# An attention block gated by an MLP, one core: the last head group in a new order, and another way through its last two units

## The chip, the cores and the metric

The kernel runs on one core of one Trainium2 chip. The metric is the device time of one execution in microseconds. The engines are called PE (TensorE), DVE (VectorE), ACT (ScalarE), POOL (GpSimd) and SP (SyncE, here only a DMA queue).

## The reference

`x` has 2048 tokens of 512 features. Its layer norm `xn` feeds two branches. One is attention with 32 heads of 128 features over a cache of 2048 keys, the other an MLP whose output gates the first.

```python
q = (xn @ wq).reshape(B, Sq, H, Dh)                       # 32 heads, Dh = 128
scores = einsum("bhqd,bhkd->bhqk", q, k_cache) * Dh**-0.5
o = einsum("bhqk,bhkd->bhqd", softmax(scores), v_cache)
s = o.reshape(B, Sq, H * Dh) @ wo                         # 4096 -> 512
h = gelu(layernorm(xn) @ w1), each quarter of its features shifted by 1 or 2 tokens
x1 = xn + h @ w2
g = silu(x1 + gelu(layernorm(x1) @ w3) @ w4)
out = x + s * g
```

Inputs and output are bf16.

## The kernel before

The MLP branch comes first; its result, twice the gate, lies in `xall` (16 token tiles of 128). Most of the time is then attention. It is cut into 128 units: 8 head groups (`g`) x 4 query blocks of 512 tokens (`qt`) x 4 heads (`hh`), in this order. Below, the 16 units of the last group are numbered 0 to 15. A unit has 8 slots (`p`), each with 256 keys. In slot `p` the kernel issues, for every engine in the order that is written (`pin` keeps it):

- `s_slot`: two matmuls of scores, transposed (keys on the partitions), into one of two double banks `psS`, and ACT's exp of both (`pT`). No maximum is subtracted.
- `pv_slot`, five slots later (`LAG`): two matmuls that add to the head's output `o`, transposed, in a bank of `psO`.
- p 0, 1: the q projection for the next unit into bank "xa" of `psX`; p 2: DVE copies it to `qT` (`q_copy`).
- p 4, p 6 and p 0 of the next unit: DVE adds up the four `pT` pieces into `acc` (`add_first`, `add_next`, `add_last`; the last one folds it twice more, to 512 columns).
- p 3: `sums` for the unit before. Four matmuls with a vector of ones sum over the partitions, into bank "xa"; DVE takes the reciprocal; SP writes it to DRAM (`dr`), and at p 4 `bcast` reads it back, spread over all partitions (`rb`).
- p 2: `norm` for the unit two before: DVE multiplies `o` by `rb` into `oT`.
- p 4, 5, 6: if a query block of a group is complete, one of its four token tiles goes through Wo (`wo_mm`, four matmuls, one per head, into bank "xm") and `wo_post`. DVE adds the result to `sacc`; in the last group DVE then multiplies by half of `xall` and adds `x` (loaded by POOL's DMA queue, `fin_load`), and SP writes the tile out.

One unit takes one token tile of the block that was finished before, so that in the last group five tiles are left when the units end; a loop does them one after the other.

PSUM has eight banks: two double ones for scores, two for `o`, "xa" and "xm".

Of the kernel before, what the change touches and what calls it, by code (L numbers as in the profile page):

```python
# [8 lines left out]
ACT = mybir.ActivationFunctionType  # L9
ALU = mybir.AluOpType  # L10
FP32 = mybir.dt.float32
BF16 = mybir.dt.bfloat16
# [5 lines left out]
def kernel(  # L18
# [15 lines left out]
    nc = tc.nc  # L34
    P = nc.NUM_PARTITIONS

    x2d = A_x.flatten_outer_dims()
    out2d = out.flatten_outer_dims()
    Sq, D = x2d.shape
    _, H, Sk, Dh = A_k_cache.shape  # L40
# [4 lines left out]
    QT = Sq // 512  # L45
# [5 lines left out]
    HG = 4  # L51
    NG = H // HG

    SPU = KC // 2
    LAG = 5
# [6 lines left out]
    pin = tc.keep_in_program_order  # L62

    def pool(name, bufs=1, space=None, **kw):
        if space is not None:
            kw["space"] = space
        return tc.tile_pool(name=name, bufs=bufs, **kw)

    ent = ctx.enter_context
    const = ent(pool("const"))  # L70
    xnT = const.tile([P, DC, Sq], BF16, name="xnT")
    xall = const.tile([P, NT, D], BF16, name="xall")
    ones_t = const.tile([P, 1], BF16, name="ones_t")
    nhalf = const.tile([P, 1], FP32, name="nhalf")
    mv1 = const.tile([P, NT, nc.vector.BN_AGGR_DIM], FP32, name="mv1")
    mv2 = const.tile([P, NT, nc.vector.BN_AGGR_DIM], FP32, name="mv2")
# [10 lines left out]
    smp = ent(pool("smp", 4))  # L87
    tokp = ent(pool("tok", 4))
    drp = ent(pool("drp", 4, bass.MemoryType.DRAM))
    psS = ent(pool("psS", 2, PSUM))  # L90
    psO = ent(pool("psO", 2, PSUM))
    psX = ent(pool("psX", 1, PSUM))
# [12 lines left out]
    def mm(out, lhsT, rhs, start, stop):  # L105
        pin(nc.tensor.matmul(out=out, lhsT=lhsT, rhs=rhs, start=start, stop=stop))  # L106

    pin(nc.vector.memset(warm[:], 0.0))
    pin(nc.vector.memset(ones_t[:], 1.0))
    pin(nc.vector.memset(nhalf[:], -0.5))  # L110
    pin(nc.gpsimd.iota(diag[:], pattern=[[-1, P]], base=0, channel_multiplier=1,
                       allow_small_or_imprecise_dtypes=True))
    pin(nc.vector.tensor_scalar(
        out=ident[:], in0=diag[:], scalar1=0.0, scalar2=None, op0=ALU.is_equal))

    units = [(g, qt, hh) for g in range(NG) for qt in range(QT) for hh in range(HG)]
    NU = len(units)
    NS = NU * SPU
    kTs, vBs, wqs, wos, oTs, st = {}, {}, {}, {}, {}, {}
# [136 lines left out]
    def q_mm(u, dcs, tag="xa"):  # L256
        g, qt, hh = units[u]
        if dcs[0] == 0:
            st[u] = dict(psq=psX.tile([P, 512], FP32, tag=tag, name="ps_q"))
        for dc in dcs:  # L260
            mm(st[u]["psq"][:], wqs[g * HG + hh][:, dc, :],
               xnT[:, dc, qt * 512:(qt + 1) * 512], dc == 0, dc == DC - 1)
# [9 lines left out]
    def s_slot(u, p):  # L272
        g, qt, hh = units[u]
        s = st[u]
        sps = psS.tile([P, 2, 512], FP32, name="ps_s")
        for j in range(2):
            kc = 2 * p + j
            kv = kTs[g * HG + hh].rearrange("d (i p j) -> d i j p", p=P, j=KJ)
            mm(sps[:, j, :], kv[:, kc // KJ, kc % KJ, :], s["qT"][:], True, True)
        if p % 2 == 0:  # L280
            s.setdefault("pT", []).append(pB.tile([P, 4, 512], BF16, tag="pT", bufs=4, name="pT"))
        jj = 2 * (p % 2)
        pin(nc.scalar.activation(  # L283
            out=s["pT"][-1][:, jj:jj + 2, :], in_=sps[:], func=ACT.Exp, scale=SCALE))

    def add_first(u):
        s = st[u]
        s["acc"] = pB.tile([P, 4, 512], BF16, tag="acc", bufs=2, name="acc")
        pin(nc.vector.tensor_tensor(  # L289
            out=s["acc"][:], in0=s["pT"][0][:], in1=s["pT"][1][:], op=ALU.add))  # L290

    def add_next(u, i):
        a = st[u]["acc"]
        pin(nc.vector.tensor_tensor(out=a[:], in0=a[:], in1=st[u]["pT"][i][:], op=ALU.add))  # L294
# [7 lines left out]
    def pv_slot(u, p):  # L302
        g, qt, hh = units[u]
        s = st[u]
        if p == 0:
            s["o"] = psO.tile([P, 512], FP32, tag="ps_o", name="ps_o")
        pT = s["pT"][p // 2]
        for j in range(2):
            kc = 2 * p + j
            mm(s["o"][:], vBs[g * HG + hh][:, kc, :], pT[:, 2 * (p % 2) + j, :], kc == 0, kc == KC - 1)  # L310
# [10 lines left out]
        pin(nc.sync.dma_start(out=s["dr"][:], in_=rc[:]))  # L321

    def bcast(u):
        st[u]["rb"] = pB.tile([P, 512], FP32, tag="rb", bufs=2, name="rb")
        pin(nc.sync.dma_start(
            out=st[u]["rb"][:], in_=st[u]["dr"][:].rearrange("p j -> (p j)").partition_broadcast(P)))

    def norm(u):
        g, qt, hh = units[u]
        s = st.pop(u)  # L330
        if hh == 0:
            oTs[(g, qt)] = pB.tile([P, HG, 512], BF16, tag="oT", bufs=2, name="oT")
        pin(nc.vector.tensor_tensor(  # L333
            out=oTs[(g, qt)][:, hh, :], in0=s["o"][:], in1=s["rb"][:], op=ALU.mult))

    wo_box = {}
    sacc = {}
# [2 lines left out]
        wos[h] = pB.tile([P, D], BF16, tag="wo", bufs=2 * HG, name="wo_h")  # L340
        pin(nc.sync.dma_start(out=wos[h][:], in_=A_wo[h * Dh:(h + 1) * Dh, :]))

    def wo_mm(g, t, hhs, ps=None):
        if hhs[0] == 0:
            wo_box[0] = psX.tile([P, D], FP32, tag="xm", name="ps_wo") if ps is None else ps
        oT = oTs[(g, t // 4)]
        ts = t % 4
        for hh in hhs:
            mm(wo_box[0][:], oT[:, hh, ts * P:(ts + 1) * P], wos[g * HG + hh][:], hh == 0, hh == HG - 1)

    fin = {}

    def fin_load(t):
        xl = tokp.tile([P, D], BF16, tag="ta", bufs=10, name="xl")
        pin(nc.gpsimd.dma_start(out=xl[:], in_=xsrc[t]))  # L355
        fin[t] = xl

    def wo_post(g, t):
        ps = wo_box.pop(0)
        if g == 0:  # L360
            sacc[t] = pS.tile([P, D], FP32, tag="sacc", bufs=NT, name="sacc")
            pin(nc.vector.tensor_copy(out=sacc[t][:], in_=ps[:]))
            return
        sa = sacc[t][:]
        pin(nc.vector.tensor_tensor(out=sa, in0=ps[:], in1=sa, op=ALU.add))  # L365
        if g < NG - 1:
            return
        xl, gl = fin.pop(t), xall[:, t, :]
        pin(nc.vector.scalar_tensor_tensor(  # L369
            out=gl, in0=sa, scalar=0.5, in1=gl, op0=ALU.mult, op1=ALU.mult))  # L370
        pin(nc.vector.tensor_tensor(out=xl[:], in0=gl, in1=xl[:], op=ALU.add))  # L371
        pin(nc.sync.dma_start(out=out2d[t * P:(t + 1) * P, :], in_=xl[:]))

# [120 lines left out]
    pB = left.enter_context(pool("pB", reuse_waits="tile"))  # L496
# [6 lines left out]
    for g in range(NG - 1):  # L503
        b = (g * QT + QT - 1) * HG
        for hh in range(HG):
            h = (g + 1) * HG + hh
# [24 lines left out]
            at(n + 4, lambda: gate_silu(t, th["a"]))  # L531

    wo_todo = deque()
    for n in range(NS + 3 * SPU):
        u, p = divmod(n, SPU)
        if u < NU:
            g, qt, hh = units[u]
            s_slot(u, p)
        m = n - LAG
        if 0 <= m < NS:  # L540
            pv_slot(*divmod(m, SPU))
        if p in (0, 1) and 4 * HG - 1 <= u < NU - 1:
            q_mm(u + 1, (2 * p, 2 * p + 1))
        if p == 0 and 1 <= u <= NU:
            add_last(u - 1)
        if p == 2 and 4 * HG - 1 <= u < NU - 1:
            q_copy(u + 1)
        if p == 2 and 2 <= u <= NU + 1:
            norm(u - 2)
            if units[u - 2][2] == HG - 1:  # L550
                gg, qq = units[u - 2][:2]
                wo_todo.extend((gg, 4 * qq + ts) for ts in range(4))
                if gg == NG - 1:
                    fin_load(4 * qq)
        if p == 3 and 1 <= u <= NU:
            sums(u - 1)
        if p == 4 and 1 <= u <= NU:
            bcast(u - 1)
        if p in (4, 5) and wo_todo:
            wo_mm(*wo_todo[0], (0, 1) if p == 4 else (2, 3))  # L560
        if p == 6 and wo_todo:
            gg, t = wo_todo.popleft()
            wo_post(gg, t)
            if gg == NG - 1 and t % 4 < 3:
                fin_load(t + 1)
        if p == 4 and u < NU:
            add_first(u)
        if p == 6 and u < NU:
            add_next(u, 2)
        held_mm(n)  # L570
        for fn in todo.pop(n, ()):
            fn()
        if not held and not todo.get(n + 1) and pS is None and n >= 4 * SPU + 5:
            right.close()
            pS = right.enter_context(pool("pS", side="right", reuse_waits="tile"))
    while wo_todo:
        gg, t = wo_todo.popleft()
        wo_mm(gg, t, (0, 1, 2, 3))
        if t not in fin:
            fin_load(t)  # L580
        wo_post(gg, t)
    left.close()
    right.close()

# [29 lines left out]
```

## Time and profile before

| | us |
|---|---|
| three runs | 1289.19, 1289.25, 1290.49; median 1289.25 |
| the profiled execution | 1289.44 |
| its span in the profile | 1287.6 |
| busy: PE, ACT, DVE, POOL | 1257.4, 1054.8, 942.5, 47.5 |
| granted PE clock, mean | 0.991 |

The span runs from the first to the last recorded instruction or transfer; the profiled execution is 1.84 us longer. Some helpers record for many callers: all matmuls and weight loads stand under L106, and are told apart by their tiles (`ps_s` scores, `ps_o` output, `ps_wo` Wo, `ps_sum` sums, `ps_q` projection). L283 is the exp, L289 `add_first`, L294 `add_next`, L299 and L300 the folds, L267 the q copy, L319 the reciprocal, L321 and L325 the write and the read of the round trip, L333 `norm`, L365, L369 and L371 the three instructions of `wo_post`, L372 the output. L167 and L168 are POOL's part of the layer norm, L177 its last DVE instruction, all in the first 76 us. A timeline line has the start, the length, the engine, the line, the operation, and in brackets the idle time before it and what ended it.

### The profile page before, as it was taken

What the parts mean: (1) busy time and instruction counts of PE and PEld (TensorE: products, weight loads), DVE (VectorE), ACT (ScalarE), POOL (GpSimd) and SP (SyncE); (2) the same over time, 40 slices, a digit from 0 to 9 for tenths busy, and PEclk for the clock granted to TensorE, in tenths of its full rate; (3) what the DMA queues carried; (4) which work ended last, traced back from release to release, by engine and by line L of the source; (5) the groups of instructions that cost most, each with busy time, mean ns of one, the idle gap of its engine ahead of it and who ended that gap; (6) DMA issues with size and microseconds to landing.
All of it is one profiled execution on the core that took longest, in us unless ns stands there. A gap on an engine that the chain in (4) does not pass through costs nothing.

```text
span 1287.6 us, 16764 instructions
## 1 busy us (share of the span) xinstructions
PE 1257.4 (98%) x6128; PEld 609.6 (47%) x6252; DVE 942.5 (73%) x1316; ACT 1054.8 (82%) x1101; POOL 47.5 (4%) x115
## 2 busy tenths in 40 slices
PE   7999999999999999999999999999999999999995
PEld 3444444444444444444444444444444444444442
DVE  6721467777777777777777777777777777778886
ACT  4344779998888888888888888888888888888882
POOL 5320000000000000000000000000000000000000
PEclk9999999999999999999999999999999999999997
DMA  9293122443144522452145423451244323442211
GB/s 209 45 172 74 21 46 50 82 91 67 41 74 77 97 34 51 90 96 46 48 83 77 79 42 59 90 95 33 55 91 78 62 51 72 85 82 43 65 43 49
DMA packets 170771, 91.57 MB, mean 71 GB/s; under 512 B 124928, under 2 KB 153088, under 8 KB 170688
## 3 DMA queue, kind: packets, MB, share of 16 engines
q1 hardware_dynamic: 166464, 84.72, 34.3%
q0 software_dynamic: 1824, 4.98, 1.7%
q8 instruction: 49, 0.80, 0.3%
q10 hardware_dynamic: 2400, 0.79, 0.2%
q14 instruction: 34, 0.28, 0.1%
HBM read 67.63 MB, written 2.36 MB: 54 GB/s over the span
## 4 chain that ended last, share of the span: by engine, by line
PE 89%; DVE 6%; DMA 2%; ACT 1%; issue 1%; POOL 0%; another core or an unknown queue 0%; SPq 0%; DVEq 0%; ACTq 0%
PE ps_s L106 36%; PE ps_o L106 35%; PE ps_wo L106 8%; PE ps_q L106 7%; DVE acc L294 2%; PE ps_m L106 2%; PE ps_sum L106 1%; ACT pT L283 1%; DVE sacc L365 1%; DVE xall L369 1%; DVE acc L299 1%; DMA kT<-in_A_k_cache_dram 1%; DVE qT L267 0%; DVE xl L371 0%; DMA xnT<-xall 0%
## 5 line engine op out<-in xcount | busy, mean ns | idle before, releaser
L283 ACT ACTIVATE pT<-ps_s 128x1024 bf16<-128x1024 f32 x1024 | 993.1, 1026 | 135.3 <-PE ps_s L106 130.4
L106 PE MATMUL ps_o<-pT,vb 128*128 128x512 bf16 x2030 | 605.0, 379 | 3.3
L106 PE MATMUL ps_s<-qT,kT 128*128 128x512 bf16 x1986 | 596.8, 380 | 3.9 <-ACT pT L283 1.2
L294 DVE TENSOR_TENSOR acc<-acc,pT 128x2048 bf16<-128x2048 bf16 x256 | 312.3, 1220 | 72.3 <-ACT pT L283 71.2
L106 PEld LDWEIGHTS <-kT 128*128 128x128 bf16 x2048 | 222.0, 113 | 203.0 <-issue 6.1
L106 PEld LDWEIGHTS <-vb 128*128 128x128 bf16 x2048 | 199.9, 98 | 225.7
L289 DVE TENSOR_TENSOR acc<-pT 128x2048 bf16<-128x2048 bf16 x128 | 156.8, 1225 | 51.2 <-ACT pT L283 51.2
L106 PE MATMUL ps_wo<-wo_h,oT 128*128 128x512 bf16 x509 | 154.5, 387 | 6.2 <-DVE sacc L365 3.1
L365 DVE TENSOR_TENSOR sacc<-ps_wo,sacc 128x512 f32<-128x512 f32 x112 | 77.4, 691 | 89.5 <-PE ps_wo L106 88.7
L106 PE MATMUL ps_q<-xnT,wq_h 128*128 128x512 bf16 x481 | 141.6, 379 | 0.2
L299 DVE TENSOR_TENSOR acc<-acc 128x1024 bf16<-128x1024 bf16 x128 | 88.5, 691 | 4.4
L333 DVE TENSOR_TENSOR oT<-ps_o,rb 128x512 bf16<-128x512 f32 x128 | 87.3, 682 | 2.6 <-DMA rb<-dr 2.6
L106 PEld LDWEIGHTS <-oT 128*128 128x128 bf16 x512 | 50.4, 99 | 70.2 <-issue 7.6
L106 PEld LDWEIGHTS <-wq_h 128*128 128x128 bf16 x512 | 50.0, 98 | 60.4 <-issue 0.3
L267 DVE CAST qT<-ps_q 128x512 bf16<-128x512 f32 x112 | 76.3, 682 | 0.0
L300 DVE TENSOR_TENSOR acc<-acc 128x512 bf16<-128x512 bf16 x128 | 54.4, 425 | 4.4
L106 PEld LDWEIGHTS <-acc 128*128 128x128 bf16 x512 | 37.6, 116 | 34.2 <-issue 4.0
L355 POOL DMA_DIRECT2D xl<-in_A_x_dram x16 | 8.7, 543 | 1137.4 <-DMA out_dram<-xl 1014.3
L106 PE MATMUL ps_s<-xn2T,w_sb 128*128 128x512 bf16 x220 | 48.6, 379 | 0.2
L106 PEld LDWEIGHTS <-w_sb 128*128 128x128 bf16 x304 | 30.0, 99 | 39.1 <-issue 7.7
L234 ACT ACTIVATE h2T<-ps_s 128x1024 bf16<-128x1024 f32 x28 | 28.7, 1024 | 24.0 <-PE ps_s L106 23.3
L319 DVE RECIPROCAL rc<-ps_sum 128x4 f32<-128x4 f32 x128 | 23.2, 181 | 21.3 <-PE ps_sum L106 7.2
(45 smaller groups left out, 332.2 us busy)
## 6 DMA issues: line engine op xcount, KB each, us to landing
rb<-dr SPq DMA_DIRECT2D x128, 256.0 KB, 4.3
vb<-in_A_v_cache_dram SPq DMA_DIRECT2D x64, 256.0 KB, 4.4
wo_h<-in_A_wo_dram SPq DMA_DIRECT2D x32, 128.0 KB, 4.2
wq_h<-in_A_wq_dram SPq DMA_DIRECT2D x28, 128.0 KB, 4.5
w_sb<-in_B_w_dram SPq DMA_DIRECT2D x9, 256.0 KB, 5.4
kT<-in_A_k_cache_dram SPq DMA_TRANSPOSE x128, 4.4
xl<-in_A_x_dram POOLq DMA_DIRECT2D x16, 128.0 KB, 2.3
dr<-rc SPq DMA_DIRECT2D x128, 2.0 KB, 1.4
```

The source lines that it names most:

```text
L106: pin(nc.tensor.matmul(out=out, lhsT=lhsT, rhs=rhs, start=start, stop=stop))
L234: pin(nc.scalar.activation(out=h2[c, f][:], in_=ps[:], func=ACT.Gelu_apprx_tanh))
L267: pin(nc.vector.tensor_copy(out=qT[:], in_=st[u].pop("psq")[:]))
L283: pin(nc.scalar.activation(out=s["pT"][-1][:, jj:jj + 2, :], in_=sps[:], func=ACT.Exp, scale=SCALE))
L289: pin(nc.vector.tensor_tensor(out=s["acc"][:], in0=s["pT"][0][:], in1=s["pT"][1][:], op=ALU.add))
L294: pin(nc.vector.tensor_tensor(out=a[:], in0=a[:], in1=st[u]["pT"][i][:], op=ALU.add))
L299: pin(nc.vector.tensor_tensor(out=a[:, 0:2, :], in0=a[:, 0:2, :], in1=a[:, 2:4, :], op=ALU.add))
L300: pin(nc.vector.tensor_tensor(out=a[:, 0, :], in0=a[:, 0, :], in1=a[:, 1, :], op=ALU.add))
L319: pin(nc.vector.reciprocal(out=rc[:], in_=ps[:]))
L333: pin(nc.vector.tensor_tensor(out=oTs[(g, qt)][:, hh, :], in0=s["o"][:], in1=s["rb"][:], op=ALU.mult))
L365: pin(nc.vector.tensor_tensor(out=sa, in0=ps[:], in1=sa, op=ALU.add))
L369: pin(nc.vector.scalar_tensor_tensor(out=gl, in0=sa, scalar=0.5, in1=gl, op0=ALU.mult, op1=ALU.mult))
```

## The change

The units of the last group are put in another order: heads 0 to 2 of query blocks 2 and 3, then all heads of blocks 0 and 1, then head 3 of blocks 2 and 3. So the two last units (`UA`, `UB`; units 14 and 15) are one head each of blocks 2 and 3. For these two blocks (`LATE`) the Wo tiles in the units sum three heads only, and are already multiplied by the gate and have `x` added, into `sacc`. The last head's share is added later.

In the last ten units a unit does a second tile, at p 0 to 2, where more than one waits (by the queue this is units 6, 8, 9 and 12). In the last group the addition of `x` is POOL's, not DVE's.

For the two last units there is no round trip through DRAM. Their outputs are copied unscaled to SBUF (`late_o`; DVE for the first, ACT in two halves for the second), go through Wo, which puts tokens on the partitions, and are scaled there by the reciprocal as a per-partition scalar. The sums for that come out of PE with tokens on the partitions (`late_sums`): 16 matmuls of one column over `acc` for unit 14, without the folds; for unit 15, 16 over `acc` of its first two pieces, 16 over the third and 16 over the fourth. The vector holds twos, which makes the factor one half. The Wo results of unit 15 go into the two bank pairs of the scores and "xa"; its first tile is scaled by ACT and multiplied and added by POOL, the other three are DVE's. Outputs go out from SP's and ACT's queues.

The four tiles of block 1 are done during unit 15 and the five slots after it, between the matmuls.

```diff
-    units = [(g, qt, hh) for g in range(NG) for qt in range(QT) for hh in range(HG)]
+    units = [(g, qt, hh) for g in range(NG - 1) for qt in range(QT) for hh in range(HG)]
+    LATE = (QT - 2, QT - 1)
+    units += [(NG - 1, qt, hh) for qt in LATE for hh in range(HG - 1)]
+    units += [(NG - 1, qt, hh) for qt in range(QT - 2) for hh in range(HG)]
+    units += [(NG - 1, qt, HG - 1) for qt in LATE]
...
-        st[u]["rb"] = pB.tile([P, 512], FP32, tag="rb", bufs=2, name="rb")
+        st[u]["rb"] = pB.tile([P, 512], FP32, tag="rb", bufs=7, name="rb")
...
-            mm(wo_box[0][:], oT[:, hh, ts * P:(ts + 1) * P], wos[g * HG + hh][:], hh == 0, hh == HG - 1)
+            mm(wo_box[0][:], oT[:, hh, ts * P:(ts + 1) * P], wos[g * HG + hh][:], hh == 0, hh == hn - 1)
...
-    def wo_post(g, t):
+    def wo_post(g, t, eng=nc.vector):
...
+        if t // 4 in LATE:
+            pin(nc.vector.scalar_tensor_tensor(
+                out=sa, in0=sa, scalar=0.5, in1=gl, op0=ALU.mult, op1=ALU.mult))
+            pin(nc.gpsimd.tensor_tensor(out=sa, in0=sa, in1=xl[:], op=ALU.add))
+            return
...
-        pin(nc.vector.tensor_tensor(out=xl[:], in0=gl, in1=xl[:], op=ALU.add))
+        pin(eng.tensor_tensor(out=xl[:], in0=gl, in1=xl[:], op=ALU.add))
...
+    def late_sums(u, src, first, last):
+        ps = st[u]["sum"]
+        for j in range(4):
+            for i, a in enumerate(src):
+                mm(ps[:, j:j + 1], a[:, j * P:(j + 1) * P], twos_t[:],
+                   first and j == 0 and i == 0, last and j == 3 and i == len(src) - 1)
...
+    def late_wo(u, ts, ps):
+        h = units[u][0] * HG + units[u][2]
+        mm(ps, st[u]["ou"][:, ts * P:(ts + 1) * P], wos[h][:], True, True)
+
+    def late_mul(u, ts, ps):
+        t = 4 * units[u][1] + ts
+        tm = pB.tile([P, D], FP32, tag="rb", bufs=7, name="tm")
+        pin(nc.vector.scalar_tensor_tensor(
+            out=tm[:], in0=ps, scalar=st[u]["rc"][:, ts:ts + 1], in1=xall[:, t, :],
+            op0=ALU.mult, op1=ALU.mult))
+        return tm
+
+    def late_act(u, ts, ps):
+        t = 4 * units[u][1] + ts
+        tm = pB.tile([P, D], FP32, tag="rb", bufs=7, name="tm")
+        pin(nc.scalar.activation(out=tm[:], in_=ps, func=ACT.Identity, scale=st[u]["rc"][:, ts:ts + 1]))
+        pin(nc.gpsimd.tensor_tensor(out=tm[:], in0=tm[:], in1=xall[:, t, :], op=ALU.mult))
+        return tm
+
+    def late_out(u, ts, tm, eng, queue):
+        t = 4 * units[u][1] + ts
+        y = tokp.tile([P, D], BF16, tag="ta", bufs=10, name="y")
+        pin(eng.tensor_tensor(out=y[:], in0=tm[:], in1=sacc[t][:], op=ALU.add))
+        pin(queue.dma_start(out=out2d[t * P:(t + 1) * P, :], in_=y[:]))
...
+    def wo_slot(part, eng=nc.gpsimd):
+        gg, t, hn = wo_todo[0]
+        if part < 2:
+            wo_mm(gg, t, (0, 1) if part == 0 else tuple(range(2, hn)), hn)
+            return
+        wo_todo.popleft()
+        wo_post(gg, t, eng)
...
+        extra = u >= NU - 10 and len(wo_todo) > 1
...
+        if p == 0:
+            twice = extra
+        if twice and p < 3:
+            wo_slot(p)
...
+    for p in range(SPU + LAG):
+        if p < SPU:
+            s_slot(UB, p)
+        pv_slot(*divmod(UB * SPU + p - LAG, SPU))
+        if p == 0:
+            add_next(UA, 3)
+        if p == 1:
+            late_ps(UA)
+            late_sums(UA, [st[UA]["acc"][:, i, :] for i in range(4)], True, True)
+            late_rc(UA)
...
+        if p in (3, 6, 8, 10):
+            wo_tile(nc.gpsimd if p < 10 else nc.vector)
+        if p == 4:
+            late_o(UA, nc.vector)
+            add_first(UB)
+        if p in (5, 7):
+            late_tile(UA, p - 5, bank(psX, "xa"))
+            late_tile(UA, p - 4, bank(psO, "ps_o"))
+        if p == 9:
+            w = [psS.tile([P, 2, 512], FP32, name="ps_s") for _ in range(2)]
+            st[UB]["sum"] = w[0][:, 0, 0:4]
+            late_sums(UB, [st[UB]["acc"][:, i, :] for i in range(4)], True, False)
+        if p == 10:
+            late_sums(UB, [st[UB]["pT"][2][:, i, :] for i in range(4)], False, False)
+        if p == 11:
+            late_sums(UB, [st[UB]["pT"][3][:, i, :] for i in range(2)], False, False)
+        if p == 12:
+            late_o(UB, nc.scalar)
+            late_sums(UB, [st[UB]["pT"][3][:, i, :] for i in range(2, 4)], False, True)
+    late_rc(UB)
+    ws = [w[0][:, 1, :], w[1][:, 0, :], w[1][:, 1, :], bank(psX, "xa")]
+    for ts in range(4):
+        late_wo(UB, ts, ws[ts])
+    tm = late_act(UB, 0, ws[0])
+    late_out(UB, 0, tm, nc.gpsimd, nc.scalar)
+    tms = {ts: late_mul(UB, ts, ws[ts]) for ts in (1, 2)}
+    late_out(UB, 1, tms[1], nc.vector, nc.sync)
+    tms[3] = late_mul(UB, 3, ws[3])
+    late_out(UB, 2, tms[2], nc.vector, nc.scalar)
+    late_out(UB, 3, tms[3], nc.vector, nc.sync)
```

More of the change, by code (lines that the diff above doesn't have):

```diff
@@ L73 @@
     ones_t = const.tile([P, 1], BF16, name="ones_t")
+    twos_t = const.tile([P, 1], BF16, name="twos_t")
     nhalf = const.tile([P, 1], FP32, name="nhalf")
@@ L109 @@
     pin(nc.vector.memset(ones_t[:], 1.0))
+    pin(nc.vector.memset(twos_t[:], 2.0))
     pin(nc.vector.memset(nhalf[:], -0.5))
@@ L341, in load_wo, with wo_mm @@
         pin(nc.sync.dma_start(out=wos[h][:], in_=A_wo[h * Dh:(h + 1) * Dh, :]))
-    def wo_mm(g, t, hhs, ps=None):
+    def wo_mm(g, t, hhs, hn):
         if hhs[0] == 0:
-            wo_box[0] = psX.tile([P, D], FP32, tag="xm", name="ps_wo") if ps is None else ps
+            wo_box[0] = psX.tile([P, D], FP32, tag="xm", name="ps_wo")
         oT = oTs[(g, t // 4)]
@@ L372, in wo_post, with late_ps, late_rc @@
         pin(nc.sync.dma_start(out=out2d[t * P:(t + 1) * P, :], in_=xl[:]))
+    def late_ps(u):
+        st[u]["sum"] = psX.tile([P, 4], FP32, tag="xa", name="ps_sum")[:]
+    def late_sums(u, src, first, last):
[4 more added lines that the diff above has]
+                   first and j == 0 and i == 0, last and j == 3 and i == len(src) - 1)
+    def late_rc(u):
+        rc = smp.tile([P, 4], FP32, tag="rl", bufs=2, name="rl")
+        pin(nc.vector.reciprocal(out=rc[:], in_=st[u]["sum"]))
+        st[u]["rc"] = rc
@@ new lines, in late_o @@
+    def late_o(u, eng):
+        s = st[u]
+        s["ou"] = pB.tile([P, 512], BF16, tag="ou", bufs=2, name="ou")
+        for c in (slice(0, 256), slice(256, 512)):
+            if eng is nc.scalar:
+                pin(eng.activation(out=s["ou"][:, c], in_=s["o"][:, c], func=ACT.Identity))
+            elif c.start == 0:
+                pin(eng.tensor_copy(out=s["ou"][:], in_=s["o"][:]))
+    def late_wo(u, ts, ps):
+        h = units[u][0] * HG + units[u][2]
+        mm(ps, st[u]["ou"][:, ts * P:(ts + 1) * P], wos[h][:], True, True)
@@ L533, with norm_queue @@
     wo_todo = deque()
-    for n in range(NS + 3 * SPU):
+    def norm_queue(u):
+        norm(u)
+        gg, qq, hh = units[u]
+        late = gg == NG - 1 and qq in LATE
+        if hh == HG - 1 - late:
+            wo_todo.extend((gg, 4 * qq + ts, HG - late) for ts in range(4))
+            if gg == NG - 1:
+                fin_load(4 * qq)
+    UA, UB = NU - 2, NU - 1
+    def wo_slot(part, eng=nc.gpsimd):
[5 more added lines that the diff above has]
+        wo_post(gg, t, eng)
+        if gg == NG - 1 and t % 4 < 3 and t + 1 not in fin:
+            fin_load(t + 1)
+    for n in range(UB * SPU):
         u, p = divmod(n, SPU)
-        if u < NU:
-            g, qt, hh = units[u]
-            s_slot(u, p)
+        extra = u >= NU - 10 and len(wo_todo) > 1
+        s_slot(u, p)
         m = n - LAG
@@ L541 @@
             pv_slot(*divmod(m, SPU))
-        if p in (0, 1) and 4 * HG - 1 <= u < NU - 1:
+        if p in (0, 1) and 4 * HG - 1 <= u:
             q_mm(u + 1, (2 * p, 2 * p + 1))
-        if p == 0 and 1 <= u <= NU:
+        if p == 0 and 1 <= u:
             add_last(u - 1)
-        if p == 2 and 4 * HG - 1 <= u < NU - 1:
-            q_copy(u + 1)
[L548 to L555, printed above, removed]
+        if p == 0:
+            twice = extra
+        if twice and p < 3:
+            wo_slot(p)
+        if p == 2 and 4 * HG - 1 <= u:
+            q_copy(u + 1)
+        if p == 2 and 2 <= u:
+            norm_queue(u - 2)
+        if p == 3 and 1 <= u:
             sums(u - 1)
-        if p == 4 and 1 <= u <= NU:
+        if p == 4 and 1 <= u:
             bcast(u - 1)
[L559 to L566, printed above, removed]
+        if p in (4, 5, 6) and wo_todo:
+            wo_slot(p - 4)
+        if p == 4:
             add_first(u)
-        if p == 6 and u < NU:
+        if p == 6:
             add_next(u, 2)
@@ L575, with wo_tile, late_tile, bank @@
             pS = right.enter_context(pool("pS", side="right", reuse_waits="tile"))
[L576 to L581, printed above, removed]
+    def wo_tile(eng):
+        for part in range(3):
+            wo_slot(part, eng)
+    def late_tile(u, ts, ps):
+        late_wo(u, ts, ps)
+        late_out(u, ts, late_mul(u, ts, ps), nc.gpsimd, nc.sync)
+    def bank(pl, tag):
+        return pl.tile([P, D], FP32, tag=tag, name="ps_w")[:]
@@ new lines @@
+    w = None
+    for p in range(SPU + LAG):
[8 more added lines that the diff above has]
+            late_rc(UA)
+        if p == 2:
+            norm_queue(UB - 2)
+            for t in range(1, 4):
+                fin_load(4 * (QT - 3) + t)
+        if p in (3, 6, 8, 10):
+            wo_tile(nc.gpsimd if p < 10 else nc.vector)
+        if p == 4:
+            late_o(UA, nc.vector)
[14 more added lines that the diff above has]
+            late_sums(UB, [st[UB]["pT"][3][:, i, :] for i in range(2, 4)], False, True)
```

## The prediction, made before the changed kernel was run

> **What bounds the kernel now.** I read the page first, then DVE's reciprocals (L319, one for each unit, so their distance is the length of a unit), then the chain of waits over the last 60 us, then the timelines of POOL and DVE. The unit numbers 0 to 15 are those of the last head group.
>
> The page: the share of the chain by engine.
>
> ```profile
> PE 89%; DVE 6%; DMA 2%; ACT 1%; issue 1%; POOL 0%; another core or an unknown queue 0%; SPq 0%; DVEq 0%; ACTq 0%
> ```
>
> PE bounds the kernel almost everywhere. The DVE timeline, reciprocals of units 4 to 7:
>
> ```profile
> 1159.92 0.18 DVE L319 RECIPROCAL rc<-ps_sum 128x4 f32<-128x4 f32 x1
> 1168.69 0.18 DVE L319 RECIPROCAL rc<-ps_sum 128x4 f32<-128x4 f32 x1
> 1177.95 0.17 DVE L319 RECIPROCAL rc<-ps_sum 128x4 f32<-128x4 f32 x1
> 1187.06 0.17 DVE L319 RECIPROCAL rc<-ps_sum 128x4 f32<-128x4 f32 x1
> ```
>
> A unit takes 8.77 us up to unit 5, then 9.26 once, then 9.10. The 8.77 is PE's own: ten back-to-back PV matmuls spread over 2.32 us, the last of them 0.38, so one comes every 0.2156 us, and 40 of them make 8.62; the four sums take the other 0.15, 0.036 each. From unit 5 on a tile of the last group costs DVE three instructions (L365, L369, L371) instead of one. The chain of waits through unit 13, start, length and work:
>
> ```profile
> 1241.23 0.27 PE ps_sum L106 x4
> ...
> 1243.68 0.45 PE ps_wo L106 x2
> ...
> 1244.15 0.70 DVE sacc L365
> ...
> 1244.88 0.70 DVE xall L369
> ...
> 1245.60 0.42 DVE xl L371
> 1246.02 1.15 DVE acc L294
> ...
> 1247.27 1.24 DVE acc L294
> ...
> 1248.53 0.70 DVE acc L299
> ...
> 1249.59 0.69 DVE qT L267
> ```
>
> It is a loop: PE's sums to the end of Wo 2.92 us, then DVE 0.73 + 0.72 + 0.42 for the tile, 1.25 and 1.26 for the two acc adds, 0.72 + 0.34 for the folds, 0.74 for the q copy, which frees the bank that the next sums need. Sum 9.10, and PE waits for it. The end of the chain:
>
> ```profile
> 1269.50 4.14 DMA rb<-dr
> ...
> 1275.80 1.88 PE ps_wo L106 x4
> ...
> 1284.45 0.42 DVE xl L371
> ```
>
> After the last scores come a DMA round trip (L321 1.38 us, L325 4.14) and five Wo tiles, each waiting for one bank. From the sums of unit 14 (1250.33) to the end of the span (1287.6) are 37.3 us.
>
> **The change, unit by unit.** The span is 1287.6 us, the profiled execution 1289.44, the median 1289.25: changes of the span are added to 1289.25. About 0.2% (2.6 us) can be told from no change.
>
> *Order of units, loads.* The same instructions, and the heads 0 to 2 start in the same units. Head 3 is first used in unit 9 instead of 3, so its K and V have more time. Cost 0. Seven rb buffers and one memset (0.06 us at the start) cost 0.
>
> *One DVE add less per tile.* L371 (0.42) goes to POOL, so the loop with one tile falls to 8.68, under PE's 8.77. A tile of three heads needs one matmul less: chain 8.46, PE 8.55.
>
> *Two tiles in one unit* (6, 8, 9, 12). The extra tile puts 0.73 + 0.72 = 1.45 on the loop ahead of the q copy, and 3 or 4 matmuls on PE. Chain 8.46 + 1.45 = 9.91 with three heads (PE 9.20), 8.68 + 1.45 = 10.13 with four (PE 9.63): DVE decides.
>
> *Sum for units 6 to 14, nothing colliding:* 9.91 three times (6, 8, 9), 8.55 twice (7, 10), 8.05 for unit 11 (no tile; PE 7.91, and exps back to back come every 0.92 us, which holds the bare slots), 10.13 (12), 8.77 twice (13, 14): 82.55 us. Before it is 1250.79 - 1168.69 = 82.10. So 12 tiles instead of 9 are done here for +0.4.
>
> *The POOL add.* No row has its like. From below: POOL's iota writes 128 elements per partition in 0.237 us, a memset of 5 takes 0.09, so 1.17 ns an element, and 512 make 0.69 with the fixed part if reads come free; from above, three streams in turn (two read, one written), 0.09 + 3 x 0.60 = 1.89. I take 1.25, between them, since a write may run beside a read. The Trainium skill's "GPSIMD Engine Reference", section 3.1, has 2.6 cycles an element for a two-input add, an estimate of 1.1 us here; no run here shows it yet, and by it each wait below is 0.15 shorter.
>
> What it does to DVE hangs on who gets SBUF first. The timelines of DVE and POOL in the first stage:
>
> ```profile
> 6.63 0.38 DVE L177 TENSOR_SCALAR xall<-xin,mv,rs 128x512 bf16<-128x512 bf16 x1
> ```
>
> ```profile
> 4.57 0.22 POOL L167 TENSOR_SCALAR ve<-mv 128x1 f32<-128x1 f32 x1 [3.21 <-DVE mv L173]
> ...
> 6.80 0.29 POOL L167 TENSOR_SCALAR ve<-mv 128x1 f32<-128x1 f32 x1 [0.48 <-DVE mv L173]
> ...
> 7.92 0.35 POOL L167 TENSOR_SCALAR ve<-mv 128x1 f32<-128x1 f32 x1 [0.18 <-DVE mv L173]
> ```
>
> Alone, L167 takes 0.22. The one at 6.80 meets L177 (to 7.01) and ends at 7.09; the one at 7.92 meets L177 (7.78 to 8.19) and ends at 8.27: POOL finished 0.08 after DVE both times, so it waited. In the loop DVE starts its next instruction 0.02 to 0.05 after the one before. I conclude that POOL, ready just after L369, finds the acc adds and folds in its way and is served when DVE reads PSUM. With one tile that is the q copy and the norm: 1249.59 to the next acc add at 1250.93 is 1.34 us, and 1.25 + 0.08 fits. With two tiles it is the second tile's sacc add (0.73), so the product after it waits 0.60. Four times (into units 6, 8, 9, 12): +2.4. Units 6 to 14: +0.4 + 2.4 = +2.8.
>
> Queues: POOL's x load (0.54, landing 2.3 later) stands behind the add, which delays only POOL. On SP the output of a (q block 0) tile waits for POOL's add, and the next unit's dr and rb wait behind it; today rb is issued at 1252.39, lands about 4.3 later (1256.7), and its norm starts at 1258.70, so 2.0 us of delay are covered.
>
> *The tail*, from the sums of unit 14. Removed: the round trip before the last two heads, their norms, the folds, five serial Wo tiles. Steps:
> 1. Sums 0.27 and four bare slots at 0.92: unit 15 starts at 3.95.
> 2. PE's program for unit 15 up to the last sums: 62 matmuls x 0.2156 = 13.4; 64 sums in runs. Such a run loads weights each time: three loads take 0.18, so 0.06 each, 3.8 (by the 0.036 of above 2.3; kept for the range). Waits: the 16 sums of unit 14 need its last acc add (its exp ends 0.7 into unit 15, add 1.25, so 0.3 late), the first late Wo needs the copy behind a tile's two instructions (0.4). 17.9, at 21.9.
> 3. Reciprocal 0.2, late Wo to the second bank 0.6: 22.7. ACT's copy (0.60 for the whole tile by L269) lies beside the last sums.
> 4. DVE: three products and three adds at 0.72: 27.0. ACT and POOL do the fourth tile: 0.6 + 2 x 1.25, ready by 26, hidden.
> 5. Today L371 ends at 1284.87 and the span at 1287.6, so 2.7 for the output: 29.7. The middle of the tail has 11 us of DVE work in 12, so collisions with POOL's seven adds may show: I put 0.8, giving 30.5.
> Tail: 30.5 - 37.3 = -6.8.
>
> Sum: +2.8 - 6.8 = **-4.0 us: 1285.3.**
>
> **Rivals.**
>
> *A. No collision at all* (DVE acc adds and POOL don't hinder each other; the rows above show only a tensor_scalar in POOL's way). +0.4 - 7.6 = -7.2: 1282.1; with cheap sums 1280.6.
>
> *B. POOL is next as soon as it waits, and then DVE waits (slower).* The add, ready after L369, waits through the first acc add; at its end POOL goes ahead, and the second acc add waits 1.25 + 0.08 = 1.33. It is on the loop wherever a tile is finished at the end of a unit: intervals 6, 7, 8, 9, 10, 12, 13, 14. 8 x 1.33 = 10.6; +0.4 + 10.6 = +11.0; the tail loses 2 (-5.6). +5.4: 1294.7. It decides from (7.2 - 2) / 8 = 0.65 us of wait per add; with the add's bounds, 0.69 and 1.89, the result is +1.0 to +10.6. For it: POOL did wait on DVE, so some way is shared; against: no DVE instruction in the first stage is seen waiting for POOL (L177 takes 0.38 to 0.41 throughout). The rule of the Trainium skill, "SBUF — State Buffer", section "Who interferes with whom", speaks for it: a DVE instruction with two SBUF inputs and a POOL instruction that reads SBUF exclude each other, and the first to start holds the way to its end. The acc adds have two such inputs, the q copy and norm do not; the trace agrees that POOL waits (0.08 after L177's end), and shows no DVE wait.
>
> *C. They share.* Each slows the other by half, 0.67 a tile end: +0.4 + 5.4 - 6.6 = -0.8: 1288.4.
>
> **How the numbers follow.** Forecast 0.35, A 0.22, B 0.35, C 0.08. Faster by over 0.2%: forecast and A, 0.57. Same: C, 0.08. Slower: B, 0.35. The forecast's own range is 1283.8 to 1287.3 (sums 1.5 less; collisions 2 more). The range must take in A and most of B: 1281.0 to 1296.0, leaving out the cheap end of A and B above 1.5 us an add, together under 0.2. Forecast and B are equally likely, but A lies on the forecast's side.
>
> **What the changed profile would show.** Reciprocals of units 6, 8, 9, 12 about 10.5 us after the one before, of 7 and 10 8.55, of 13 and 14 8.77. POOL's adds (L378, L382) beginning, or ending, under the q copy (L273) and the norm (L339); the acc adds (L300) at 1.22 with no gap ahead. By B the second L300 starts over 1 us after the first has ended, and units 7 and 13 take 9.9 or more. From unit 14's sums to the end about 30 us, with no DMA in the chain but the last output. I am wrong if the middle stretch is over 88 us (B), or the tail over 33.

## The result and the profile after

| | before | after |
|---|---|---|
| median of 18 runs, us | 1289.80 | 1287.31 |
| range of the runs, us | 1288.94 to 1292.83 | 1286.90 to 1288.29 |
| span of the profiled execution, us | 1287.6 | 1285.4 |
| units 6 to 14, reciprocal to reciprocal, us | 82.10 | 87.83 |
| last unit's reciprocal of that stretch to the end, us | 36.8 | 29.2 |

The ratio is 0.9978, with a 95% interval of 0.9972 to 0.9985: faster by 0.22%. Two large changes of opposite sign stand behind it. The middle stretch is 5.7 us longer, the tail 7.6 shorter. The remaining 0.3 us lie ahead of unit 6 (unit 5's reciprocal at 1168.37 instead of 1168.69); over the runs below that moment scatters from 1167.92 to 1170.07, so nothing is read from it. Each experiment below is compared with the kernel before in the same set of runs, so the time of before differs a little from set to set.

The page of the changed kernel, share of the chain by engine:

```profile
PE 91%; DVE 6%; ACT 1%; DMA 1%; issue 1%; POOL 0%; DVEq 0%; ACTq 0%
```

PE still carries the chain, and the 5.5 us of the round trip are gone from it. DVE's timeline, reciprocals of units 5, 6, 7 and 14 (now L325):

```profile
1168.37 0.18 DVE L325 RECIPROCAL rc<-ps_sum 128x4 f32<-128x4 f32 x1
1179.05 0.17 DVE L325 RECIPROCAL rc<-ps_sum 128x4 f32<-128x4 f32 x1
1188.26 0.17 DVE L325 RECIPROCAL rc<-ps_sum 128x4 f32<-128x4 f32 x1
...
1256.20 0.17 DVE L325 RECIPROCAL rc<-ps_sum 128x4 f32<-128x4 f32 x1
```

Unit 6 takes 10.68 us, unit 7, with one tile, 9.21: longer than the 9.11 before the change, although DVE has one instruction less in it. The chain of waits between the reciprocals of units 6 and 7 shows where:

```profile
1181.30 0.70 DVE sacc L371
...
1182.03 0.69 DVE sacc L376
1182.72 1.15 DVE acc L300
...
1183.96 2.01 DVE acc L300
...
1185.99 0.70 DVE acc L305
```

The second acc add took 1.24 us before and takes 2.01 here. POOL's timeline (start, length):

```profile
1172.43 1.90 POOL L378 TENSOR_TENSOR sacc<-sacc,xl 128x512 f32<-128x512 f32 x1 [1055.20 <-ACT pT L289]
...
1178.18 1.15 POOL L378 TENSOR_TENSOR sacc<-sacc,xl 128x512 f32<-128x512 f32 x1 [3.34 <-ACT pT L289]
...
1183.47 1.40 POOL L378 TENSOR_TENSOR sacc<-sacc,xl 128x512 f32<-128x512 f32 x1 [3.64 <-PE ps_s L107]
```

The first and the last belong to tiles that end ahead of the acc adds. The last one starts during the first acc add, which ends at 1183.87, is open until 1184.87, and the second acc add beside it is long; the first one lies the same way against the acc adds of 1172.11 to 1175.42 and is open for 1.90. The middle one, of a unit's second tile, starts under the q copy (1177.86) and the norm and takes 1.15; q copy and norm keep their 0.68. In the tail, the chain of waits:

```profile
1261.59 0.55 PE ps_sum L107 x16
...
1266.82 1.72 DVE acc L295
...
1275.74 1.31 DVE xl L382
...
1277.20 0.82 PE ps_s L107 x3
```

Sixteen sums of one column take 0.55 us. From the first tile of unit 15 (1264.80) to the last reciprocal the chain is DVE's but for one Wo tile, and two of DVE's additions are drawn out: the acc add from 1.23 to 1.72, the x addition from 0.42 to 1.31, both beside POOL's adds.

The granted PE clock of the tail also differs. Two lines of the view by stretches, the tail before and after (at the end of a line stand the clock, the DMA share and GB/s):

```profile
1250.80:1287.60 36.80, 23.07 (x92) 8.96 (x91) 24.16 (x38) 11.74 (x13) 0.00 (x0) 0.74 0.19 47
```

```profile
1256.20:1285.40 29.20, 19.93 (x146) 9.59 (x143) 20.68 (x29) 12.88 (x15) 12.61 (x9) 0.88 0.22 64
```

Before, the clock was 0.50 from 1274 on, and a Wo tile there took 1.88 us (1275.80 in the prediction's lines); in the changed kernel's tail the clock is 1.00 up to the last reciprocal, and the Wo tile at 1263.90 takes 0.88. Two such tiles lie on the chain of before, so some 2 us of the 7.6 go with the clock, an estimate from these rows. What lowers the clock was not tried.

### The profile page after: what moved, and what is told of

The parts are those of the page before. It is cut to its first block, busy times and chain, and to the rows that moved or that the text cites. A ratio compares the mean times of both kernels' runs of the same rounds, so it can differ in the third digit from the quotient of the medians.

```text
span 1285.4 us, 17040 instructions
## 1 busy us (share of the span) xinstructions
PE 1261.3 (98%) x6308; PEld 611.3 (48%) x6308; DVE 945.1 (74%) x1305; ACT 1055.6 (82%) x1104; POOL 78.2 (6%) x136
## 4 chain that ended last, share of the span: by engine, by line
PE 91%; DVE 6%; ACT 1%; DMA 1%; issue 1%; POOL 0%; DVEq 0%; ACTq 0%
PE ps_s L107 37%; PE ps_o L107 35%; PE ps_wo L107 8%; PE ps_q L107 8%; DVE acc L300 2%; PE ps_m L107 2%; PE ps_sum L107 1%; DVE sacc L371 1%; ACT pT L289 1%; DVE acc L305 0%; DVE qT L273 0%; DMA xnT<-xall 0%; DVE tm L418 0%; DVE sacc L376 0%; DVE xall L380 0%
## 5 line engine op out<-in xcount | busy, mean ns | idle before, releaser
L107 PE MATMUL ps_s<-qT,kT 128*128 128x512 bf16 x2048 | 609.6, 379 | 1.3 <-ACT pT L289 1.2
L300 DVE TENSOR_TENSOR acc<-acc,pT 128x2048 bf16<-128x2048 bf16 x254 | 316.3, 1245 | 75.1 <-ACT pT L289 74.3
L107 PE MATMUL ps_wo<-wo_h,oT 128*128 128x512 bf16 x504 | 149.9, 379 | 0.1
L107 PE MATMUL ps_q<-xnT,wq_h 128*128 128x512 bf16 x512 | 147.8, 379 | 0.0
L378 POOL TENSOR_TENSOR sacc<-sacc,xl 128x512 f32<-128x512 f32 x8 | 11.3, 1410 | 1083.2 <-ACT pT L289 1058.5
L107 PE MATMUL ps_sum<-ones_t,acc 128*128 128x1 bf16 x504 | 33.6, 171 | 6.5 <-DVE qT L273 6.5
```

Source lines behind the costliest of these rows:

```text
L378: pin(nc.gpsimd.tensor_tensor(out=sa, in0=sa, in1=xl[:], op=ALU.add))
```

## The experiments

Theory T: POOL's add, once it waits, gets its turn when DVE's running two-input instruction ends, and DVE's next one waits. Rival W: the long acc add has another cause in the new order.

**1. No POOL adds in the units.** What is left out, in `wo_post`:

```diff
-            pin(nc.gpsimd.tensor_tensor(out=sa, in0=sa, in1=xl[:], op=ALU.add))
             return
```

and likewise for block 0, whose tiles go out without x.

> Left out: the addition of x to the 12 token tiles that are finished in units 5 to 13 (nothing takes its place on any engine). Theory T (turns): a POOL add that waits gets SBUF when the running acc add ends, and the next acc add then stands for about 0.8 us. Then without the adds the second acc add is back at 1.23, units 7 and 10 take 8.55 and units 13 and 14 8.77, units 6 to 14 together 82.5 us instead of 87.8, and the time is about 1282.0. Rival W (the acc add's 2.0 us comes from something else in the new order, such as exps that end later): second acc add 2.0 as in the changed kernel, time about 1287.3.

1281.54 us against 1289.16, ratio 0.9937 (0.9925 to 0.995). DVE's two acc adds together:

```profile
1172.06 2.55 DVE L300 TENSOR_TENSOR acc<-acc,pT 128x2048 bf16<-128x2048 bf16 x2
```

2.55 instead of 3.31. Units 6 to 14 take 82.14 us. W falls: the long add is POOL's doing. Without the POOL adds the stretch takes what it took before the change (82.14 against 82.10), with 12 tiles in it instead of 9.

**2. The adds on DVE.**

```diff
-            pin(nc.gpsimd.tensor_tensor(out=sa, in0=sa, in1=xl[:], op=ALU.add))
+            pin(nc.vector.tensor_tensor(out=sa, in0=sa, in1=xl[:], op=ALU.add))
...
-    def wo_slot(part, eng=nc.gpsimd):
+    def wo_slot(part, eng=nc.vector):
```

> The 12 adds of units 5 to 13 go to DVE (128x512, float out 0.69 for blocks 2 and 3, bf16 0.42 for block 0). T: the acc adds are 1.23 again, but the adds stand on the loop: at the end of a unit 0.72 instead of 0.80 five times, 0.45 instead of 0.80 three times; where a unit does a second tile 0.72 three times and 0.45 once instead of nothing. Sum +1.2: about 1288.5. Had POOL's add cost what the prediction took (hidden with one tile, 0.60 with two), moving it to DVE would cost 4 to 5 us: 1292. W: the acc add stays 2.0 and the adds come on top, 1295 or more.

1289.77 against 1289.16, ratio 1.0007 (0.9998 to 1.0016): 0.0029 above the changed kernel's ratio, 3.7 us, where T said +1.2 and the hidden add +4 to 5. Units 6 to 14 take 89.20 (1257.27 - 1168.07), +1.4 as T has it; the acc adds are 2.55 together. The profiled execution (1288.22) was the fastest of its 11 runs, which reach up to 1292.26, and its span is only 1.0 longer than the changed kernel's, so the size stays loose. The sign does not: on POOL, even with the wait, the adds are cheaper than on DVE.

**3. Product and add at p 2 of the next unit**, for the tile that ends at p 6:

```diff
+        if p == 2:
+            while deferred:
+                deferred.pop(0)()
         if twice and p < 3:
             wo_slot(p)
```

> Same work. Of a tile that ends at p 6 only the sacc add stays there; DVE's product and POOL's add are issued at p 2 of the next unit, ahead of the q copy, so POOL's add meets the q copy and the norm, not the acc adds. T: the two acc adds at 1.23 each, no stretch, units 6 to 14 about 82.5 to 83.5 us (in a unit with two tiles POOL's two adds, 2.3 us, reach 1 us into the first acc add of the next unit, behind which DVE is idle for 0.9): 1282 to 1283, faster than the changed kernel by 4 to 5. If POOL's add slows DVE wherever it lies: as the changed kernel, 1287.

1286.13 against 1289.16, ratio 0.9976 (0.9966 to 0.9986): as the changed kernel. Both expectations were too simple. Units 7, 10, 13 and 14 came down to 8.77 to 9.01. But units 6, 8, 9 and 12 stayed at 10.6 to 10.9; DVE's and POOL's timelines there:

```profile
1177.37 1.30 DVE L385 SCALAR_TENSOR_TENSOR sacc<-sacc,xall 128x512 f32<-128x512 f32 x1
```

```profile
1176.97 1.15 POOL L387 TENSOR_TENSOR sacc<-sacc,xl 128x512 f32<-128x512 f32 x1 [1056.34 <-DVE sacc L385]
```

Now the first tile's add runs in front of the second tile's product, which reads two tiles from SBUF as the acc adds do, and takes 1.30 instead of 0.69. That is T again, at another instruction; besides, the second acc add now waits 0.58 for its exp.

**4. One part alone:** the kernel before, with its 16 additions of x on POOL.

```diff
-        pin(nc.vector.tensor_tensor(out=xl[:], in0=gl, in1=xl[:], op=ALU.add))
+        pin(nc.gpsimd.tensor_tensor(out=xl[:], in0=gl, in1=xl[:], op=ALU.add))
```

> The kernel before with one part of the change alone: the 16 additions of x go from DVE to POOL, at the place where they stand. T: in units 6 to 14 the loop loses 0.42 and gains 0.80: 9.48 instead of 9.10, +3.4; at the end the last add is POOL's 1.15 instead of 0.42, +0.8: 1293.5 against 1289.3 to 1289.8. By the prediction's reckoning (hidden): the loop falls to 8.77, -3.0, and +0.8 at the end: 1287.

1297.69 against 1289.16, ratio 1.0063 (1.0051 to 1.0076). Units 7 to 14 take 9.41 instead of 9.10: 9.10 - 0.42 + 0.76 = 9.44, so this is T's price. Units 6 to 14 together are 2.75 us longer, and the rest, some 6 us, is in the tail and was expected by nobody. POOL's timeline there:

```profile
1283.51 1.14 POOL L371 TENSOR_TENSOR xl<-xall,xl 128x512 bf16<-128x512 bf16 x1 [2.20 <-DMA xl<-in_A_x_dram]
...
1287.38 1.14 POOL L371 TENSOR_TENSOR xl<-xall,xl 128x512 bf16<-128x512 bf16 x1 [2.22 <-DMA xl<-in_A_x_dram]
```

The load of x for the next tile stands in POOL's queue behind the add: add 1.14, issue 0.55, landing 2.2, so 3.87 us a tile instead of 2.65; four such steps and 0.7 for the last add make 5.6. In the changed kernel the last block's loads are issued ahead (`fin_load` for three tiles at p 2), which avoids this.

**5. A POOL instruction that only writes.**

```diff
-            pin(nc.gpsimd.tensor_tensor(out=sa, in0=sa, in1=xl[:], op=ALU.add))
+            pin(nc.gpsimd.memset(sa, 0.0))
```

> Left out: the addition of x to the 12 tiles of units 5 to 13; in the place of each POOL add stands a POOL memset of the same 128x512 tile, which reads nothing (it waits for the product as the add did; these tiles are lost). If DVE's wait comes from POOL's reading (T, and the rule of the Trainium skill, SBUF — State Buffer, section Who interferes with whom, says that an instruction that only writes is in nobody's way here): the two acc adds take 1.23 each and the time is that of the kernel without adds, 1281.5 to 1282. If any POOL instruction over SBUF does it: the second acc add is longer by about the memset's length, some 0.4 to 0.6, and the time 1285.

1281.31 against 1289.02, ratio 0.9939 (0.9925 to 0.9953): as without any add. POOL's and DVE's timelines:

```profile
1172.06 0.52 POOL L378 MEMSET sacc<- 128x512 f32 x1 [1055.20 <-ACT pT L289]
```

```profile
1171.82 2.55 DVE L300 TENSOR_TENSOR acc<-acc,pT 128x2048 bf16<-128x2048 bf16 x2
```

It ended at 1172.58, before the first acc add did, and the acc adds kept their length. (For block 0 the edit likewise puts a memset in the add's place.) What collides is POOL's reading; a POOL instruction that reads one tile only was not tried. The rule of the Trainium skill, "SBUF — State Buffer", section "Who interferes with whom", holds here in both halves: a POOL read and a two-input DVE instruction exclude each other, a POOL write and one do not.

**6. Unit 15's sums by DVE again**, two acc adds and the folds in place of 48 sums:

```diff
-            late_sums(UB, [st[UB]["acc"][:, i, :] for i in range(4)], True, False)
+            add_next(UB, 2)
+            add_last(UB)
...
-            late_sums(UB, [st[UB]["pT"][3][:, i, :] for i in range(2, 4)], False, True)
+            late_sums(UB, [st[UB]["acc"][:, 0, :]], True, True)
```

> Unit 15's sums as in the kernel before: two more acc adds and two folds by DVE (1.23 + 1.23 + 0.69 + 0.42 = 3.6 us) and 4 sum matmuls on PE instead of 48 (about 1.5 us less at 0.034 each). T: the changed kernel's tail is bound by DVE from the first tile of unit 15 to the last reciprocal, so nearly all of the 3.6 shows: 1290 to 1291. Rival: PE binds the tail, as the prediction's steps had it: PE's 1.5 us come off and the adds find room, 1286 to 1287.

1293.06 against 1289.02, ratio 1.0031 (1.0019 to 1.0043); 5.8 us above the changed kernel by the medians and 6.8 by the ratios, more than the 3.6 of T; the rival's 1286 to 1287 is out. In its chain of waits the two acc adds take 2.22 and 2.11 and the fold 1.53, where 1.23, 1.23 and 0.69 were counted: 2.7 us more, beside POOL's adds for unit 14. From unit 14's own sums to the last reciprocal it takes 5.2 us longer than the changed kernel, and from there to the end 1.1 (9.5 instead of 8.4), at a granted clock of 0.50 instead of 0.60. Up to the last reciprocal, then, DVE binds the tail, not PE.

**7. Products behind the q copy.** Only the sacc add, which reads PSUM, stays in its place; product and POOL add follow the next q copy.

```diff
             q_copy(u + 1)
+            if deferred:
+                deferred.popleft()()
...
             sums(u - 1)
+            while deferred:
+                deferred.popleft()()
```

> Same work. In the units, of a tile only the sacc add stays in its place (p 6 or p 2); product and POOL add come behind the next q copy: the tile of p 6 between q copy and norm, that of p 2 behind the reciprocal. The products leave the loop (0.72 or 1.45) and POOL's adds meet PSUM readers, or the first acc add, behind which DVE was idle for 0.9. T: one tile 8.55 to 8.77, two tiles 9.2 (three heads) to 9.65 (PE's own), units 6 to 14 together 80 to 81 us: 1279.5 to 1281. If the first acc add of a two-tile unit is late by POOL's second add and the loop feels it: 0.5 more four times, 1282.

1280.53 against 1289.02, ratio 0.9933 (0.9921 to 0.9946). Units 6 to 14 take 80.55 us, 7.3 less than in the changed kernel. DVE's timeline, the two products of unit 6:

```profile
1178.64 0.68 DVE L385 SCALAR_TENSOR_TENSOR sacc<-sacc,xall 128x512 f32<-128x512 f32 x1
...
1179.93 1.24 DVE L385 SCALAR_TENSOR_TENSOR sacc<-sacc,xall 128x512 f32<-128x512 f32 x1
```

The second still meets POOL's first add (1.24), but stands where DVE would wait for the next Wo tile.

**8. Unit 15 through the round trip**, on top of experiment 6:

```diff
-            late_o(UB, nc.scalar)
-            late_sums(UB, [st[UB]["acc"][:, 0, :]], True, True)
+            sums(UB)
+            bcast(UB)
```

> The kernel with unit 15's sums by DVE, and unit 15 also through the round trip again: reciprocal, write to DRAM, spread read, norm of the output into SBUF by DVE, then the same late Wo and products (scalar one half instead of the reciprocal). To compare with the kernel with DVE sums (1293.1 against 1289.0 before). T: the trip lies bare, as in the kernel before: 1.38 + 4.14 + a norm of 0.69 in place of a matmul that waits for the reciprocal anyway, +6: 1299. Rival: the late outputs of units 14 and block 1 on POOL cover part of it, +3: 1296.

1299.49 against 1288.49, ratio 1.0084 (1.007 to 1.0097): 6.4 us above experiment 6. The trip lies bare in its chain of waits, and costs what the kernel before paid:

```profile
1283.68 4.12 DMA rb<-dr
```

**9. Two moves in the tail**, on top of experiment 7: the last x addition behind the third product, and the sums in the bank pair of the last Wo tile.

```diff
-    ws = [w[0][:, 1, :], w[1][:, 0, :], w[1][:, 1, :], bank(psX, "xa")]
+    ws = [w[1][:, 0, :], w[1][:, 1, :], bank(psX, "xa"), w[0][:, 1, :]]
...
+    last_add[0]()
     late_out(UB, 3, tms[3], nc.vector, nc.sync)
```

> The kernel with products behind the q copy, and two moves in the tail: DVE's last x addition (1.31 us in the changed kernel, 0.9 of it waiting for POOL) goes from in front of the last reciprocal to behind the third product, and unit 15's sums share a bank pair with the last Wo tile instead of the first, whose matmul then does not wait for the reciprocal. T: the reciprocal comes 1.2 earlier, 0.43 is paid later: about 0.8 to 1.0 less than the kernel without the two moves. If PE or the output transfers bind the end: no difference.

1279.85, ratio 0.9934 (0.9922 to 0.9947): not to be told from 0.9933. The reciprocal did come earlier: 13.90 us after the reciprocal of unit 14's own sums (1254.25 to 1268.15) instead of 15.01. But what followed grew by about as much, 0.96 us to the end of the span. DVE's timeline, the first product:

```profile
1269.77 0.75 DVE L435 SCALAR_TENSOR_TENSOR tm<-ps_s,rl,xall 128x512 f32<-128x512 f32 x1 [1.44 <-ACT tm L443]
```

It starts 1.62 us after the reciprocal; in experiment 7 it was 1.07, behind a wait for PE. By the profile DVE now waits for ACT, which reads the first late Wo tile; with the new order that tile shares a bank pair with the second one. The x addition behind the third product adds 0.41. The expectation had counted only the latter. Unit 13's norm shows another wait:

```profile
1255.93 0.69 DVE L339 TENSOR_TENSOR oT<-ps_o,rb 128x512 bf16<-128x512 f32 x1 [1.49 <-DMA rb<-dr]
```

Experiment 7 has the same one (1.48), the changed kernel has none. Since the adds end later, so do block 0's outputs, which stand on SP ahead of the reciprocal's write: that write was issued 1.0 us after its reciprocal and landed 2.6 later.

**10. Outputs behind the spread read**, on top of experiment 9:

```diff
             bcast(u - 1)
+            while outs:
+                outs.popleft()()
```

> The kernel with products behind the q copy and the two tail moves, and one more: the output transfers of block 0's tiles are issued on SP behind the spread read (p 4) instead of ahead of the reciprocal's write. In the run without this the last write was issued 1.0 after its reciprocal and landed 2.6 later, behind an output, and the last norm waited 1.49 for the read. T: that wait goes, 0.5 to 1.0 less than 1279.85 (ratio to before 0.9925 to 0.993). If the norm is not on the path (the Wo tile has room): no difference.

1279.31 against 1288.49, ratio 0.9926 (0.9913 to 0.994). The wait at that norm fell from 1.49 to 0.31, but the next one, for the Wo tile behind it, grew from 0.48 to 1.43. The ratio's interval overlaps those of 7 and 9, so the gain of this step is not shown. It is the best version tried, and lies clear of the changed kernel's 0.9972 to 0.9985.

**11. POOL's add in two halves.**

```diff
-            pin(nc.gpsimd.tensor_tensor(out=sa, in0=sa, in1=xl[:], op=ALU.add))
+            for c in (slice(0, 256), slice(256, 512)):
+                pin(nc.gpsimd.tensor_tensor(out=sa[:, c], in0=sa[:, c], in1=xl[:, c], op=ALU.add))
```

> The changed kernel, but POOL's add for the eight tiles of blocks 2 and 3 is two instructions of 256 columns. Turns for each instruction: the first half gets in between the two acc adds, the second behind the second acc add, ahead of the fold: second acc add longer by about 0.4 instead of 0.77, the fold (L305, 0.69) longer by about 0.4, time as the changed kernel, 1287. If POOL keeps its place over both halves: second acc add about 2.0 to 2.1, fold 0.69. If the wait is a fixed price for each meeting, whatever the width: acc add 2.0 and fold 1.45, loop longer by 0.77 five times, 1291.

1286.43 against 1289.27, ratio 0.9978 (0.9968 to 0.9988). The chain of waits:

```profile
1173.73 1.51 DVE acc L300
...
1175.27 1.05 DVE acc L305
```

The second acc add is longer by 0.27 and the fold by 0.35. So POOL and DVE take turns instruction by instruction, and the wait grows with the width of POOL's instruction.

## Why the prediction came out as it did

The measured time lies in the range and on the forecast's side, at about 60% of the forecast gain (2.5 us against 4.0). That it came so near was luck in part: the middle stretch was 2.9 us worse than forecast (+5.7 against +2.8), the tail 0.8 better (-7.6 against -6.8), and the range was 15 us wide. With 87.83 us the middle stayed just below the 88 that the prediction had named as its sign of being wrong. Point by point, with units 6 to 14 as lengths in us:

| unit | nothing colliding | forecast | after | no adds (exp. 1) |
|---|---|---|---|---|
| 6 | 9.91 | 10.51 | 10.68 | 9.92 |
| 7 | 8.55 | 8.55 | 9.21 | 8.44 |
| 8 | 9.91 | 10.51 | 10.52 | 9.87 |
| 9 | 9.91 | 10.51 | 10.67 | 9.76 |
| 10 | 8.55 | 8.55 | 9.20 | 8.43 |
| 11 | 8.05 | 8.05 | 7.82 | 7.97 |
| 12 | 10.13 | 10.73 | 10.90 | 10.34 |
| 13 | 8.77 | 8.77 | 9.42 | 8.64 |
| 14 | 8.77 | 8.77 | 9.41 | 8.77 |
| sum | 82.55 | 84.95 | 87.83 | 82.14 |

*The loop* was right: with the collisions taken away (experiment 1) every unit lies within 0.21 us of the column that has none, and the two-tile units are DVE's, not PE's.

*The POOL add* was taken at 1.25 and takes 1.14 to 1.16 undisturbed. The estimate of 1.1 from the Trainium skill's figure ("GPSIMD Engine Reference", section 3.1) is nearer; the run agrees with it.

*Who gets SBUF first* is the step that failed. The prediction reasoned from POOL finishing 0.08 after L177 and DVE starting 0.02 to 0.05 after its previous instruction that POOL would be passed over until DVE reads PSUM. The row behind L177 shows why that did not follow:

```profile
6.93 0.69 DVE L172 BATCH_NORM_STATS2 bn<-xin 128x6 f32<-128x512 bf16 x1
```

DVE's next instruction there reads one tile only, so no DVE instruction with two SBUF inputs stood against the waiting POOL, and the rows could not tell who goes first. The runs show rival B's mechanism: POOL goes in as soon as the running acc add ends, and the next one waits (experiments 1, 5 and 11). The two-tile units came out near the forecast, 10.5 to 10.9, by the wrong cause: not a product that waits 0.60, but an acc add that waits 0.77.

*Rival B's price* was mis-sized: 1.33 a meeting, where 0.76 to 0.77 were measured. Over all acc adds L300 is busy 316.3 us with the adds and 310.2 without (experiment 1), 6.1 us for eight meetings instead of the 10.6 that B counted. Of POOL's 1.15 us, then, about 0.4 does not keep DVE out, so "to its end", as the prediction has the rule, is not borne out in full. In the rows of unit 7 POOL ends 1.00 after the first acc add (1183.87 to 1184.87), and the second one, at its usual 1.24, would have to start at 1184.73, some 0.14 before POOL's end. Whether that is POOL's writing after its last read was not tried.

*The rival by which they share* had the total nearly right (1288.4) with a mechanism that the rows speak against: the first acc add keeps its 1.15 us on the chain while POOL's add is open beside it, and only the next one is late. A time that fits is no proof of the story behind it.

*The tail* was forecast at 30.5 us from unit 14's sums and took 29.7. Inside, two errors offset each other. The 64 sums were priced at 0.06 and take 0.034, so that PE is done 20.1 after those sums instead of 21.9. But DVE, which the steps had beside PE, is the bound: the reciprocal comes at 21.2, 1.2 after PE's last sum, behind an x addition drawn out by POOL. The collisions were allowed 0.8; 0.5 (acc add) and 0.9 (x addition) are seen on the chain. The round trip, 5.5 us in the chain of before, was worth 6.4 in experiment 8, with the norm that goes with it.

*SP's queue* was costed as covered with 2.0 us to spare, and it is so in the changed kernel; experiments 7 and 9 show a wait of 1.5 us there when the adds come later.

## What to carry to other kernels

Moving an elementwise add to an idle POOL is not free where DVE runs instructions with two SBUF inputs: the question is which DVE instruction comes next. Put POOL's readers beside DVE instructions that read PSUM, and first take off the loop whatever only needs to be done at some time: here the products and adds behind the q copy were worth more than twice the whole change (6.8 us by the medians, 5.8 by the ratios, against 2.5). A queue that also loads (POOL) or also stores (SP) delays those transfers with its wait; follow them in the new place.

## What the runs showed of the hardware

- A POOL add of two SBUF tiles (128x512, 1.15 us alone) that becomes ready during a DVE add of two SBUF tiles waits for its end and then makes the next such DVE instruction 0.77 us longer; in two halves, 0.27 and 0.35 on the next two. A POOL memset of the same tile (0.52 us) did neither.
- A POOL add of 128x512 took 1.14 us at least with a float and a bf16 input and a float output, and 1.14 with bf16 throughout. With two float inputs and a bf16 output (L433, in the tail of the changed kernel) it took 1.27 at least.
- Runs of one-column matmuls with a new 128x128 weight load each take 0.034 us apiece (0.55 for 16), no more than single ones between wide matmuls (0.036).
- In units 6 to 14 of before (1168.7 to 1250.8) the granted PE clock was 1.00; from 1274 on in its tail it was 0.50, and four Wo matmuls took 1.88 us there instead of 0.88 in the tail of the changed kernel.
